# Two blocks' convolution moved from two to all four 64x64 tiles of TensorE

## The chip, the cores and the metric

The kernel runs on one core of one Trainium2 chip. The metric is the time of one execution in device microseconds (us).

## The reference, cut to what matters

A causal depthwise convolution with 7 taps per head (softmax over the taps), then a product, an exact GELU and a second product, for 8 x 4096 tokens of 192 channels.

```python
w = softmax(weight)                       # 8 heads x 7 taps, 24 channels a head
x_pad = concatenate([zeros(B, 6, D), x])  # per sequence
out[b, s, h] = sum_k w[h, k] * x_pad[b, s + k, h]
...
h = out.reshape(32768, 192) @ w_in        # 192 x 2048
g = 0.5 * h * (1 + erf(h / sqrt(2)))
return g @ w_out                          # 2048 x 192
```

## The kernel before

Tokens are halved over partitions: partitions 0 to 63 hold 64 channels of the first half of the tokens, partitions 64 to 127 the same channels of the second half. Three channel groups p = 0, 1, 2 lie along the free axis. Work goes in blocks n; the first six have 256 tokens a half. For all blocks but the two first, VectorE does the convolution. For blocks 0 and 1 TensorE does it, as 7 accumulating matmuls per group and half, each with the diagonal 64x64 matrix of one tap. I call the matmuls that stand together behind one product a bundle. `win` and `wout` are the two weight matrices in SBUF, `xc` holds the result of the convolution, and the halo is the 6 tokens before a block that its taps reach back to.

```python
def pconv(n, p, k):                      # TensorE: group p, tap k of block n
    ...                                  # waits for the cast, the diagonals, the halo
    for hf in range(2):                  # token half = row half = column half
        r = slice(64 * hf, 64 * hf + 64)
        ins = t.matmul(
            bank(CONVB[n][p], r, w), dg[r, d0 : d0 + 64], xTb[PC[n]][r, x0 : x0 + w],
            start=(k == KS - 1), stop=(k == 0),
            tile_position=(64 * hf, 64 * hf),
        )
    if k == 0:
        ins.then_inc(S_PC)

for p in range(NP):                      # block 1's groups go behind products 4, 5, 6 of block 0
    behind[0, 4 + p] = [(1, p, k) for k in range(KS - 1, -1, -1)]
```

Two of the four tiles work: (0, 0) and (64, 64). The results are copied from PSUM to `xc`, by ScalarE for block 0 and by VectorE for block 1. VectorE is one queue in order, and the place of block 1's copies in it matters below:

```python
diag(0); diag(1)                         # diagonals of groups 0 and 1
for p in range(NP): trans(0, p)
diag(2)                                  # diagonals of group 2
dup(0)                                   # two copies of win's first slice
dup(1); dup(2)
for p in range(NP): trans(1, p)
for p in range(NP): cast(1, p)

# copy p of block 1 stands before operation 0, 3 or 5 of block 2;
# operations 0 to 2 of block 2 are its transposes, which wait for its load
side = [((2, (0, 3, 5)[p]), conv_out, 1, p) for p in range(NP)]
```

The first product of block n (`mm1`, line 703) needs all of `xc`; it is followed by GELUs on ScalarE (line 631) and by the second product (line 734 or 767), which needs `wout`.

Of the kernel before, what the change touches and what calls it, by code (L numbers as in the profile page):

```python
# [6 lines left out]
AF = mybir.ActivationFunctionType  # L7
# [4 lines left out]
def bass_lightweight_conv__then__act_gelu_exact_kernel(  # L12
# [8 lines left out]
    H, KS = weight.shape  # L21
# [7 lines left out]
    TB = 512  # L29
# [4 lines left out]
    PC = {0: 0, 1: 1}  # L34
# [66 lines left out]
    def sem(name):  # L101
        return es.enter_context(nc.semaphore(name))
# [4 lines left out]
    with es:  # L107
# [37 lines left out]
        S_CAST = [sem("S_CAST%d" % i) for i in range(len(PC))]  # L145
        S_PC = sem("S_PC")
        S_PCE = sem("S_PCE")
        S_DUPE = sem("S_DUPE")
        S_HALO = sem("S_HALO")
        S_TR = sem("S_TR")  # L150
# [12 lines left out]
            return ob[r, 512 * (b % 4) : 512 * (b % 4) + w]  # L163


        CONVB = {0: [0, 1, 2], 1: [3, 0, 1]}

        NCV = NP * KS
        FQ = F // 8
# [3 lines left out]
        def cvd(n):  # L173

            return NCV * sum(m not in PC for m in range(n + 1))

        def pce(n, p):

            return NP * PC[n] + p + 1


        HC = [0]
# [156 lines left out]
        @block.gpsimd  # L339
        def _(g):  # L340
            def win_in(c0, c1, sm):
                for hf in range(2):
                    g.dma_start(  # L343
                        ap(win, 64 * hf * NP * F + c0, [[NP * F, 64], [F, NP], [1, c1 - c0]]),
                        ap(wint, hf * FH + c0, [[NP * F, 64], [F, NP], [1, c1 - c0]]),
                    ).then_inc(sm, 16)

            g.wait_ge(S_MSET, 1)
            for hf in range(2):
                m = idb[64 * hf : 64 * hf + 64, :]  # L350
                g.affine_select(
                    out=m,
                    in_=m,
                    compare_op=ALU.is_equal,
                    fill=0.0,
                    base=0,
                    pattern=[[-1, 64]],
                    channel_multiplier=1,
                ).then_inc(S_IDN)
            for i in range(3):  # L360
                win_in(FP[i], FP[i + 1], S_WIN[i])

            def halo(n):
                if n == 0:

                    t = xTb[0]
                    g.memset(
                        ap(t, 0, [[NP * XB, 128], [XB, NP], [32, HB]]), 0.0
                    ).then_inc(S_HALO)
                    for p in range(NP):  # L370
                        g.wait_ge(S_TR, p + 1)
                        g.tensor_copy(
                            ap(t, p * XB + 1, [[NP * XB, 128], [32, HB], [1, 31]]),
                            ap(
                                xT[0],
                                p * XW + HX + WS[0] - HL,
                                [[NP * XW, 128], [32, HB], [1, 31]],
                            ),
                        ).then_inc(S_HALO)
                    return  # L380

                t, tw = (xTb[1], XB) if n in PC else (xT[n % 2], XW)
                dst = ap(t, HF, [[NP * tw, 128], [tw, NP], [1, HB]])
                if n >= 2:
                    if n - 2 in PC:
                        g.wait_ge(S_PCE, pce(n - 2, NP - 1))
                    else:
                        g.wait_ge(S_CV, cvd(n - 2))
                if OFF[n] % SEQ == 0:
                    g.memset(dst, 0.0).then_inc(S_HALO)  # L390
                    return
                g.wait_ge(S_TR, NP * n)
                if n == 1:
                    src = ap(
                        xT[0],
                        HX + WS[0] - HL + 31,
                        [[NP * XW, 128], [XW, NP], [32, HB]],
                    )
                else:
                    src = ap(  # L400
                        xT[(n - 1) % 2],
                        HF + WS[n - 1],
                        [[NP * XW, 128], [XW, NP], [1, HB]],
                    )
                g.tensor_copy(dst, src).then_inc(S_HALO)  # L405

            g.wait_ge(S_IDN, 2)
            halo(0)
            g.dma_start(
                ap(wout, 0, [[NF * C, 128], [C, NF], [1, C]]),  # L410
                ap(woutt, 0, [[C, 128], [128 * C, NF], [1, C]]),
            ).then_inc(S_WOUT, 16)
            halo(1)
            for n in range(2, NB):
                halo(n)

        @block.vector
        def _(v):
# [62 lines left out]
                    ap(xT[n % 2], p * XW + HX, [[NP * XW, 128], [1, WS[n]]]),  # L481
                ).then_inc(S_CAST[PC[n]])

            def conv_out(n, p):
                v.wait_ge(S_PC, pce(n, p))
                v.tensor_copy(
                    xc[n % 2][:, p * TB : p * TB + WS[n]], bank(CONVB[n][p], w=WS[n])
                ).then_inc(S_PCE)

            def trans(n, p):  # L490
                w = WS[n]
                if p == 0:
                    if xin_at(n) > 0:
                        v.wait_ge(S_XIN[n % NX], xin_at(n))
                    if n >= 2 and n - 2 in PC:
                        v.wait_ge(S_PCE, pce(n - 2, NP - 1))
                    elif n >= 2:
                        v.wait_ge(S_CV, cvd(n - 2))
                    if n >= 1:
                        v.wait_ge(S_HALO, HC[n])  # L500
                v.transpose(  # L501
                    ap(xT[n % 2], p * XW + HX, [[NP * XW, 128], [1, w]]),
                    ap(
                        xin[n % NX],
                        p,
                        [[TB // 32 * DQ, 128], [D if n == 0 else DQ, w // 32], [NP, 32]],
                    ),
                ).then_inc(S_TR)
# [38 lines left out]
            diag(1)  # L547
            for p in range(NP):
                trans(0, p)
            diag(2)  # L550
            dup(0)
            dup(1)
            dup(2)
            for p in range(NP):
                trans(1, p)
            for p in range(NP):
                cast(1, p)

            side = [((2, (0, 3, 5)[p]), conv_out, 1, p) for p in range(NP)]
            for n in range(M0, M1):  # L560
                for j, at in enumerate([(n + 2, 18), (n + 3, 6), (n + 3, 9)]):
                    side.append((at, evac_t, v, n, j))
# [16 lines left out]
        def _(a):  # L579
# [10 lines left out]
                accum_out=wsm[:, 0:1],  # L590
            ).then_inc(S_ACTP)
            a.activation(out=hot[:, 1:2], in_=warm[0:1, 0:1], func=AF.Gelu).then_inc(S_HOT)
            for p in range(NP):
                a.wait_ge(S_TR, p + 1)
                a.activation(  # L595
                    out=ap(xTb[0], p * XB + HL, [[NP * XB, 128], [1, WS[0]]]),
                    in_=ap(xT[0], p * XW + HX, [[NP * XW, 128], [1, WS[0]]]),
                    func=AF.Copy,
                ).then_inc(S_CAST[0])
            for p in range(NP):  # L600
                a.wait_ge(S_PC, p + 1)
                a.activation(
                    out=xc[0][:, p * TB : p * TB + WS[0]],
                    in_=bank(CONVB[0][p], w=WS[0]),
                    func=AF.Copy,
                ).then_inc(S_PCE)

            due = {(1, 6): [(0, 0)]}
            for m in range(NA):
# [32 lines left out]
        def _(t):  # L642
# [1 line left out]
            for i in range(16):  # L644
                t.matmul(hp[1][:, 0:512], warm[:, 0:128], warm[:, :])  # L645

            def pconv(n, p, k):

                w = WS[n]
                if k == KS - 1:  # L650
                    t.wait_ge(S_CAST[PC[n]], p + 1)
                    if n == 0:
                        t.wait_ge(S_DG, p + 1)
                if k == KS - 2:
                    t.wait_ge(S_HALO, HC[n] + 2 + p if n == 0 else HC[n + 1])
                for hf in range(2):
                    r = slice(64 * hf, 64 * hf + 64)
                    d0 = (p * KS + k) * 64
                    x0 = p * XB + (32 * k if n == 0 else HF + k)
                    ins = t.matmul(  # L660
                        bank(CONVB[n][p], r, w),
                        dg[r, d0 : d0 + 64],
                        xTb[PC[n]][r, x0 : x0 + w],
                        start=(k == KS - 1),
                        stop=(k == 0),
                        tile_position=(64 * hf, 64 * hf),
                    )
                if k == 0:
                    ins.then_inc(S_PC)

            taps = [(p, k) for p in range(NP) for k in range(KS - 1, -1, -1)]
            for p, k in taps:
                pconv(0, p, k)

            behind = {}
            for p in range(NP):
                behind[0, 4 + p] = [(1, p, k) for k in range(KS - 1, -1, -1)]

            def mm1(n, i):
                w, c = WS[n], NCH[n]  # L680
# [2 lines left out]
                    t.wait_ge(S_GELU, u - 1)  # L683
                if i == 0:
                    if n in PC:
                        t.wait_ge(S_PCE, pce(n, NP - 2))
                    else:
                        t.wait_ge(S_CV, cvd(n))
                if n == 0 and i in (0, 2, 4):
# [2 lines left out]
                for cc in range(c):  # L692
                    f0 = 128 * CH[i * c + cc]
                    for p in range(NP):
                        if n in PC and i == 0 and cc == 0 and p == NP - 1:
                            t.wait_ge(S_PCE, pce(n, p))
                        for hf in range(2):
                            r = slice(64 * hf, 64 * hf + 64)
                            fw = 64 if M0 < n <= M1 else 128
# [158 lines left out]
```

## Time and profile before

| | before |
|---|---|
| median of the first 3 runs | 686.01 us (685.57 to 686.14) |
| profiled run | 684.97 us, span 683.2 us |
| TensorE busy | 676.7 us, 99% of the span |
| convolution matmuls | 84, 5.3 us busy |
| first GELU starts | 11.04 us |
| first use of `wout` | 20.32 us |

Times in the profile are counted from the start of the span. Those of the table are from the timeline; in a chain a piece counts only from the end of the piece before it, so its start can lie up to 0.2 us later (20.49 for the 20.32 here). A line of the timeline gives start, us, engine, line, operation, output and input, and in brackets the idle time before it and what ended it.

```profile
17.15 1.33 DVE L501 STREAM_TRANSPOSE xT<-xin 128x256 f32<-128x256 f32 x3 [0.90 <-DMA xin<-in_x_dram]
...
19.23 0.42 DVE L486 CAST xc<-ob 128x256 bf16<-128x256 f32 x1
```

The transposes of block 2 wait 0.90 us for a load, and the last copy of block 1 stands behind them. Here the copy ends at 19.65 and TensorE does not wait for it: the wait costs nothing in this run.

### The profile page before, as it was taken

How to read it: one execution, taken by the hardware profiler on the slowest of the kernel's cores; microseconds unless marked ns; L12 is line 12 of the kernel's file. 1: busy time of each engine (PE TensorE's matmuls, PEld its weight loads, DVE VectorE, ACT ScalarE, POOL GpSimd, SP SyncE). 2: the span in 40 equal slices, each digit the busy share in tenths (PEclk: the TensorE clock that was granted, in tenths of full speed). 3: DMA queues.
4: the chain of work that ended last, by engine and by line, in shares of the span. 5: the costliest groups of instructions: out<-in, count | busy, mean ns of one | idle time of the engine just before them, and what ended most of it. 6: DMA issues, size and time to landing. Idle time of an engine off the chain costs nothing.

```text
span 683.2 us, 27246 instructions
## 1 busy us (share of the span) xinstructions
PE 676.7 (99%) x12548; PEld 411.2 (60%) x12548; DVE 564.3 (83%) x914; ACT 534.0 (78%) x540; POOL 20.4 (3%) x51
## 2 busy tenths in 40 slices
PE   8999999999999999999999999999999999999998
PEld 4899655555555555555555555555555555555557
DVE  6999979888889888898888898888898888988611
ACT  6788987777787877777877878777778777778772
POOL 4000000000000000000000000000000000000000
PEclk9999999999999999999999999999999999999999
DMA  9345422244431244432334422344422444320123
GB/s 180 74 108 121 91 60 57 46 89 95 94 91 46 55 94 95 94 78 41 73 94 95 94 61 46 84 95 95 93 49 51 94 95 95 76 47 23 48 49 94
DMA packets 133970, 54.00 MB, mean 79 GB/s; under 512 B 128480, under 2 KB 133728, under 8 KB 133856
## 3 DMA queue, kind: packets, MB, share of 16 engines
q1 hardware_dynamic: 129872, 49.93, 32.1%
q0 software_dynamic: 3312, 1.57, 1.8%
q8 instruction: 98, 1.61, 1.0%
q10 hardware_dynamic: 672, 0.76, 0.4%
q14 instruction: 16, 0.13, 0.1%
HBM read 28.66 MB, written 25.17 MB: 79 GB/s over the span
## 4 chain that ended last, share of the span: by engine, by line
PE 96%; ACT 2%; DVE 1%; issue 0%; DMA 0%; ACTq 0%
PE hp L703 48%; PE ob L767 42%; PE ob L734 5%; ACT gT L631 2%; PE ob L660 1%; DMA wsb<-in_weight_dram 0%; DVE dg L453 0%; ACT osb L228 0%; DVE wcol L445 0%; DVE osb L270 0%; DVE xT L501 0%; ACT xTb L595 0%; ACT wex L585 0%; DVE osb L239 0%; DVE wch L439 0%
## 5 line engine op out<-in xcount | busy, mean ns | idle before, releaser
L631 ACT ACTIVATE gT<-hp 128x1024 bf16<-128x1024 f32 x512 | 523.4, 1024 | 132.7 <-PE hp L703 129.5
L703 PE MATMUL hp<-xc,win 64*64 64x512 bf16 (+2 forms) x6048 | 418.9, 366 | 1.0 <-ACT gT L631 0.7
L767 PE MATMUL ob<-gT,wout 64*64 64x512 bf16 x5376 | 366.7, 376 | 0.0
L531 DVE SCALAR_TENSOR_TENSOR acc<-xT,wcol,acc 128x512 f32<-128x512 f32 (+1 forms) x495 | 315.0, 710 | 0.0
L703 PEld LDWEIGHTS hp<-xc,win 64*64 64x64 bf16 (+1 forms) x6048 | 188.8, 106 | 134.7 <-ACT gT L631 2.3
L767 PEld LDWEIGHTS ob<-gT,wout 64*64 64x64 bf16 x5376 | 173.3, 118 | 121.7
L270 DVE STREAM_TRANSPOSE osb<-ob 128x512 f32<-128x512 f32 x84 | 74.4, 889 | 101.4 <-PE ob L767 101.4
L501 DVE STREAM_TRANSPOSE xT<-xin 128x512 f32<-128x512 f32 (+1 forms) x105 | 78.5, 807 | 0.9 <-DMA xin<-in_x_dram 0.9
L531 DVE SCALAR_TENSOR_TENSOR xc<-xT,wcol,acc 128x512 bf16<-128x512 f32 (+1 forms) x99 | 65.2, 716 | 0.0
L734 PE MATMUL ob<-wout,gT 64*128 64x192 bf16 x1024 | 52.2, 243 | 0.3
L734 PEld LDWEIGHTS ob<-wout,gT 64*128 64x128 bf16 x1024 | 43.6, 94 | 6.3 <-PE ob L734 0.6
L524 DVE TENSOR_SCALAR acc<-xT,wcol 128x512 f32<-128x512 f32 (+1 forms) x99 | 40.7, 467 | 1.1
L405 POOL COPY xT<-xT 128x18 f32<-128x18 f32 x30 | 12.7, 423 | 531.2 <-DVE xT L501 525.4
L241 ACT ACTIVATE osb<-ob 128x192 f32<-128x192 f32 x4 | 1.3, 331 | 9.5 <-PE ob L734 9.5
L239 DVE COPY osb<-ob 128x192 f32<-128x192 f32 x4 | 1.4, 358 | 8.4 <-PE ob L734 8.4
L660 PE MATMUL ob<-xTb,dg 64*64 64x256 bf16 x84 | 5.3, 272 | 1.1 <-ACT xTb L595 1.1
L645 PE MATMUL hp<-warm 128*128 128x512 bf16 x16 | 5.0, 482 | 1.3 <-DVE warm L419 1.3
L228 ACT ACTIVATE osb<-ob 128x384 f32<-128x384 f32 x12 | 5.8, 485 | 0.0
L660 PEld LDWEIGHTS ob<-xTb,dg 64*64 64x64 bf16 x84 | 4.3, 107 | 2.3 <-ACT xTb L595 1.6
L645 PEld LDWEIGHTS hp<-warm 128*128 128x128 bf16 x16 | 1.8, 118 | 4.0 <-issue 1.9
L464 DVE COPY win<-win 64x768 bf16<-64x768 bf16 (+1 forms) x6 | 3.7, 620 | 0.2
L343 POOL DMA_DIRECT2D win<-in_moe_w_in_dram x6 | 3.9, 652 | 0.0
(31 smaller groups left out, 16.4 us busy)
## 6 DMA issues: line engine op xcount, KB each, us to landing
out_dram<-osb SPq DMA_DIRECT2D x122, 192.0 KB, 3.1
xin<-in_x_dram SPq DMA_DIRECT2D x116, 192.0 KB, 4.0
xin<-in_x_dram SPq DMA_DIRECT2D x20, 96.0 KB, 3.3
wout<-in_moe_w_out_dram POOLq DMA_DIRECT2D x1, 768.0 KB, 10.3
win<-in_moe_w_in_dram POOLq DMA_DIRECT2D x4, 96.0 KB, 4.1
win<-in_moe_w_in_dram POOLq DMA_DIRECT2D x2, 192.0 KB, 4.7
out_dram<-osb SPq DMA_DIRECT2D x8, 48.0 KB, 1.7
out_dram<-osb ACTq DMA_DIRECT2D x4, 96.0 KB, 2.1
```

Of the source, the lines that this page charges most:

```text
L228: e.activation(out=dst, in_=src, func=AF.Copy).then_inc(S_EVA)
L270: v.transpose(ap(osb[m % 2], j, [[8 * C, 128], [C // 2, TB // 32], [NP, 32]]), bank(ring(m, j)),).then_inc(S_EV)
L405: g.tensor_copy(dst, src).then_inc(S_HALO)
L501: v.transpose(ap(xT[n % 2], p * XW + HX, [[NP * XW, 128], [1, w]]), ap(xin[n % NX], p, [[TB // 32 * DQ, 128], [D if n == 0 else DQ, w // 3 ...
L524: ins = v.tensor_scalar(a, src, wk, None, ALU.mult)
L531: ins = v.scalar_tensor_tensor(dst, src, wk, a, op0=ALU.mult, op1=ALU.add)
L631: a.activation(out=ap(gT[n % 2], i * c * 2 * w, dst), in_=ap(hp[u % 2], 0, src), func=AF.Gelu,).then_inc(S_GELU)
L645: t.matmul(hp[1][:, 0:512], warm[:, 0:128], warm[:, :])
L660: ins = t.matmul(bank(CONVB[n][p], r, w), dg[r, d0 : d0 + 64], xTb[PC[n]][r, x0 : x0 + w], start=(k == KS - 1), stop=(k == 0), tile_positi ...
L703: ins = t.matmul(hp[u % 2][fo : fo + fw, o : o + w], win[r, f1 : f1 + fw], xc[n % 2][r, p * TB : p * TB + w], start=(p == 0), stop=(p == N ...
L734: ins = t.matmul(bank(bb[sub], w=C), gT[m % 2][r, c0 : c0 + 128], wout[r, CH[i] * C : (CH[i] + 1) * C], start=(ph == 0 and i == 0), stop=( ...
L767: ins = t.matmul(bank(ring(m, j), slice(64 * h, 64 * h + 64), w), ap(wout, 64 * hf * NF * C + CH[i] * C + j, [[NF * C, 64], [NP, 64]],), g ...
```

## The change

The intent is to use the two idle tiles. Groups 0 and 1 run side by side: group 0 on the straight tiles, group 1 on the crossed ones, where the first token half's result lands in the second half's partitions and the other way round. The copies out of PSUM put the halves back. Group 2 is cut in two parts of 128 columns, one straight and one crossed. With six pieces to copy instead of three, the copies are shared anew: in block 0 ScalarE takes four and VectorE the two crossed ones of group 1. ScalarE also builds group 2's diagonals, which VectorE did before. In block 1 all six copies stay on VectorE, and they now stand ahead of block 2's transposes. The code is cut where `...` stands.

```diff
+        def kinds(n):
+            w = WS[n]
+            return [(0, 0, 0, w), (1, 1, 0, w), (2, 0, 0, w // 2), (2, 1, w // 2, w // 2)]
+        PIECES = [(0, None), (1, 0), (1, 1), (2, None), (3, 0), (3, 1)]
+        PA = (0, 3, 4, 5)
 ...
             for p in range(NP):
                 trans(0, p)
-            diag(2)
             dup(0)
+            conv_out(v, 0, 1)
+            conv_out(v, 0, 2)
             dup(1)
             dup(2)
 ...
             for p in range(NP):
                 cast(1, p)
-
-            side = [((2, (0, 3, 5)[p]), conv_out, 1, p) for p in range(NP)]
+            for j in range(len(PIECES)):
+                conv_out(v, 1, j)
+
+            side = []
 ...
+            for k in range(KS):          # ScalarE: diagonals of group 2
+                a.activation(out=dg[:, d0 : d0 + 64], in_=idb[:, :], func=AF.Copy,
+                             scale=wcol[:, c0 : c0 + 1]).then_inc(S_DGA)
 ...
                 for hf in range(2):
+                    ho = hf ^ ex
-                        bank(CONVB[n][p], r, w),
+                        bank(kd, slice(64 * ho, 64 * ho + 64), w),
-                        tile_position=(64 * hf, 64 * hf),
+                        tile_position=(64 * hf, 64 * ho),
 ...
+            order = [0] * 4 + [1, 0] * 3 + [1, 2] * 4 + [3, 2] * 3 + [3] * 4
 ...
+            behind = {
+                (0, 4): [(1, kd, k) for k in taps for kd in (0, 1)],
+                (0, 5): [(1, kd, k) for k in taps for kd in (2, 3)],
+            }
```

More of the change, by code (lines that the diff above doesn't have):

```diff
@@ L147, in bass_lightweight_conv__then__act_gelu_exact_kernel @@
         S_PCE = sem("S_PCE")
+        S_PCA = sem("S_PCA")
+        S_DGA = sem("S_DGA")
         S_DUPE = sem("S_DUPE")
@@ L163, in bank, with conv_out, wait_pc @@
             return ob[r, 512 * (b % 4) : 512 * (b % 4) + w]
-        CONVB = {0: [0, 1, 2], 1: [3, 0, 1]}
+        def kinds(n):
[3 more added lines that the diff above has]
+        PA = (0, 3, 4, 5)
+        def conv_out(e, n, j):
+            kd, h = PIECES[j]
+            p, ex, c0, w = kinds(n)[kd]
+            e.wait_ge(S_PC, 4 * PC[n] + kd + 1)
+            ro = slice(0, 128) if h is None else slice(64 * h, 64 * h + 64)
+            ri = ro if not ex else slice(64 - 64 * h, 128 - 64 * h)
+            dst = xc[n % 2][ro, p * TB + c0 : p * TB + c0 + w]
+            src = bank(kd, ri, w)
+            if n == 0 and j in PA:
+                e.activation(out=dst, in_=src, func=AF.Copy).then_inc(S_PCA)
+            else:
+                e.tensor_copy(dst, src).then_inc(S_PCE)
+        def wait_pc(e, n, p):
+            if n == 0:
+                e.wait_ge(S_PCA, (1, 1, len(PA))[p])
+                if p >= 1:
+                    e.wait_ge(S_PCE, 2)
+            else:
+                e.wait_ge(S_PCE, 2 + (1, 3, 6)[p])
         NCV = NP * KS
@@ L175, in cvd @@
             return NCV * sum(m not in PC for m in range(n + 1))
-        def pce(n, p):
-            return NP * PC[n] + p + 1
         HC = [0]
@@ L385, in halo @@
                     if n - 2 in PC:
-                        g.wait_ge(S_PCE, pce(n - 2, NP - 1))
+                        wait_pc(g, n - 2, NP - 1)
                     else:
@@ L482, in cast @@
                 ).then_inc(S_CAST[PC[n]])
-            def conv_out(n, p):
-                v.wait_ge(S_PC, pce(n, p))
-                v.tensor_copy(
-                    xc[n % 2][:, p * TB : p * TB + WS[n]], bank(CONVB[n][p], w=WS[n])
-                ).then_inc(S_PCE)
             def trans(n, p):
@@ L495, in trans @@
                     if n >= 2 and n - 2 in PC:
-                        v.wait_ge(S_PCE, pce(n - 2, NP - 1))
+                        wait_pc(v, n - 2, NP - 1)
                     elif n >= 2:
@@ L592, in _ @@
             a.activation(out=hot[:, 1:2], in_=warm[0:1, 0:1], func=AF.Gelu).then_inc(S_HOT)
+            a.wait_ge(S_PRO, 10)
+            a.wait_ge(S_IDN, 2)
+            for k in range(KS):
+                d0 = ((NP - 1) * KS + k) * 64
+                c0 = (NP - 1) * 32 + k
+                a.activation(
+                    out=dg[:, d0 : d0 + 64],
+                    in_=idb[:, :],
+                    func=AF.Copy,
+                    scale=wcol[:, c0 : c0 + 1],
+                ).then_inc(S_DGA)
             for p in range(NP):
@@ L599, in _ @@
                 ).then_inc(S_CAST[0])
-            for p in range(NP):
-                a.wait_ge(S_PC, p + 1)
-                a.activation(
-                    out=xc[0][:, p * TB : p * TB + WS[0]],
-                    in_=bank(CONVB[0][p], w=WS[0]),
-                    func=AF.Copy,
-                ).then_inc(S_PCE)
+            for j in PA:
+                conv_out(a, 0, j)
             due = {(1, 6): [(0, 0)]}
@@ L645, in _, with pconv @@
                 t.matmul(hp[1][:, 0:512], warm[:, 0:128], warm[:, :])
-            def pconv(n, p, k):
-                w = WS[n]
+            def pconv(n, kd, k):
+                p, ex, c0, w = kinds(n)[kd]
                 if k == KS - 1:
@@ L652, in pconv @@
                     if n == 0:
-                        t.wait_ge(S_DG, p + 1)
+                        if p < NP - 1:
+                            t.wait_ge(S_DG, p + 1)
+                        else:
+                            t.wait_ge(S_DGA, KS)
                 if k == KS - 2:
@@ L656, in pconv @@
                 for hf in range(2):
+                    ho = hf ^ ex
                     r = slice(64 * hf, 64 * hf + 64)
                     d0 = (p * KS + k) * 64
-                    x0 = p * XB + (32 * k if n == 0 else HF + k)
+                    x0 = p * XB + (32 * k if n == 0 else HF + k) + c0
                     ins = t.matmul(
-                        bank(CONVB[n][p], r, w),
+                        bank(kd, slice(64 * ho, 64 * ho + 64), w),
                         dg[r, d0 : d0 + 64],
@@ L669, in pconv @@
                     ins.then_inc(S_PC)
-            taps = [(p, k) for p in range(NP) for k in range(KS - 1, -1, -1)]
-            for p, k in taps:
-                pconv(0, p, k)
-            behind = {}
-            for p in range(NP):
-                behind[0, 4 + p] = [(1, p, k) for k in range(KS - 1, -1, -1)]
+            taps = range(KS - 1, -1, -1)
+            seq = {kd: [(0, kd, k) for k in taps] for kd in range(4)}
+            order = [0] * 4 + [1, 0] * 3 + [1, 2] * 4 + [3, 2] * 3 + [3] * 4
+            for kd in order:
+                pconv(*seq[kd].pop(0))
+            behind = {
+                (0, 4): [(1, kd, k) for k in taps for kd in (0, 1)],
+                (0, 5): [(1, kd, k) for k in taps for kd in (2, 3)],
+            }
             def mm1(n, i):
@@ L685, in mm1 @@
                     if n in PC:
-                        t.wait_ge(S_PCE, pce(n, NP - 2))
+                        wait_pc(t, n, NP - 2)
                     else:
@@ L695, in mm1 @@
                         if n in PC and i == 0 and cc == 0 and p == NP - 1:
-                            t.wait_ge(S_PCE, pce(n, p))
+                            wait_pc(t, n, p)
                         for hf in range(2):
```

## The prediction

> **What bounds the kernel now.** I read the page first (busy shares, chain, groups), then the chain in order of time over the first 21 us, then the same stretch engine by engine, because the change touches only the two first blocks of 256 tokens a half.
>
> ```profile
> PE 676.7 (99%) x12548; PEld 411.2 (60%) x12548; DVE 564.3 (83%) x914; ACT 534.0 (78%) x540; POOL 20.4 (3%) x51
> PE 96%; ACT 2%; DVE 1%; issue 0%; DMA 0%; ACTq 0%
> L660 PE MATMUL ob<-xTb,dg 64*64 64x256 bf16 x84 | 5.3, 272 | 1.1 <-ACT xTb L595 1.1
> ```
>
> TensorE sets the time: 99% busy, 96% of the chain, full clock. The matmuls that the change rewrites (L660, the convolution as diagonal matmuls) are 84 of 12548 and 5.3 us of 683.2. So 5.3 us, 0.8%, bounds what their work can give: a verdict past 2% is out of reach unless something stalls for over 13 us. What remains is the sign and size of a change of about 1 us. Every shift of TensorE early on reaches the end one for one, as the later chain is PE behind PE; the wait on GELUs near 73 to 82 us is relative to earlier work and moves along.
>
> The chain of the first 21 us (start, us, what):
>
> ```profile
> 5.33 1.16 DVE dg L453 x2
> 6.50 0.44 DVE xT L501
> 6.96 0.42 ACT xTb L595
> 7.42 2.48 PE ob L660 x42
> 9.96 0.40 PE hp L703 x4
> 10.38 0.63 PE hp L703 x8
> 11.04 1.94 ACT gT L631 x2
> 12.99 1.03 ACT gT L631
> 14.07 0.83 PE hp L703 x12
> 14.89 0.88 PE ob L660 x14
> 15.78 0.76 PE hp L703 x12
> 16.54 0.88 PE ob L660 x14
> 17.43 0.76 PE hp L703 x12
> 18.19 0.88 PE ob L660 x14
> 19.07 1.42 PE hp L703 x24
> 20.49 0.50 PE ob L734 x12
> ```
>
> The reader should see three stages. Block 0's convolution runs 7.42 to 9.90 and releases the first product (9.96; its last third waits for the last copy until 10.38). From 11.04 to 14.07 three GELUs of about 1.0 us each set the pace. From 14.07 to 20.49 it is TensorE again: product, convolution of block 1, product, and so on.
>
> The other engines meanwhile:
>
> ```profile
> 8.28 3.88 DVE L464 COPY win<-win 64x768 bf16<-64x768 bf16 x6
> 9.95 0.39 ACT L602 ACTIVATE xc<-ob 128x256 bf16<-128x256 f32 x1 [0.38 <-PE ob L660]
> 18.41 0.39 DVE L486 CAST xc<-ob 128x256 bf16<-128x256 f32 x1
> SPq L288 <- DMA wout<-in_moe_w_out_dram: 7.9, 1, 7.9
> ```
>
> VectorE duplicates win without a gap from 8.28 to 12.16. A copy out of PSUM takes 0.39 us for 256 columns. The sync queue's wait on wout ends when its next load is issued at 18.68, so wout has landed by then; the first second-product matmul (20.32) does not wait for it now.
>
> **What the Trainium skill says.** "TensorE: Matmul & The Clock Gate", Part 3 (The mechanism), says matmuls on different tiles run concurrently with starts about 4 ns apart. The trace agrees for two tiles: 42 matmuls of 256 columns in 2.48 us are 59 ns each, 118 ns a pair, against about 107 ns for one stream of 256 columns at 2.4 GHz. The same page, Part 1 (Wait — 56ns, not 53.3ns?), gives a floor of about 25 ns between matmul starts; nothing in the trace is dense enough to test it (the closest are the 64x192 matmuls, 41 ns apart in 12 per 0.50 us). "ScalarE: Activation LUTs", What ACT_TABLE_LOAD costs, says that a per-partition pointer operand adds about 93 ns to an activation and that activations back to back overlap by about 93 ns. The trace: 0.20 us for 1x1 without a pointer, 0.30 for 8x7 with one, and five GELUs of 1.02 in 4.92 us, an overlap nearer 50 ns. "SBUF — State Buffer", on the shared port pair, says VectorE in its two-port modes and GpSimd lock each other out. The trace fits: the second win copy takes 1.06 us while GpSimd generates wout's descriptors, its like 0.45.
>
> **The change, part by part.**
>
> (a) Work on TensorE. Two whole groups (kinds 0 and 1, 256 columns) now run on the straight and the crossed tiles, and the third group is cut into two of 128 columns. Per block 56 matmuls instead of 42. If a set of four takes what a pair takes now, that is 118/4 = 29.5 ns each. I use it for the 128-column ones too, as half of it would pass the 25 ns floor. So 28 matmuls cost 28 x 29.5 = 0.83 us, what 14 cost now (14 x 59 = 0.83), and a block costs two such bundles, not three.
>
> (b) Seven activations on ScalarE build the last diagonals. Each: 0.20 + 0.10 for the pointer + 64 columns x 0.85 ns (from (417 - 200)/256) = 0.355, less 50 to 93 ns of overlap, so 0.26 to 0.31 us; seven take 1.85 to 2.1 us from 5.35, when wcol is ready. They end at about 7.3, but the first cast could start at 6.96: 0.34 us late. The three casts, 0.37 apart, end near 8.4 instead of 8.2.
>
> (c) Block 0. TensorE starts at 7.76 instead of 7.42: 4 pairs alone 0.47, 3 sets of four 0.36 (8.59), 4 sets 0.48 (9.07, kind 1 done), 3 sets 0.36 (9.43, kind 2 done), 8 matmuls of kind 3 0.24, end 9.67. VectorE, without its third diagonal, starts win's first two copies at 7.7 instead of 8.28; at the 1.54 us they take now they end at 9.25. Then the two crossed copies, 0.42 each: 9.67 and 10.09. ScalarE's 128-column copies (0.20 + 128 x 0.85 ns = 0.31 with rounding and release) end near 10.3. So the first product starts near 10.1 instead of 9.96, its last third near 10.3 instead of 10.38, and the first GELU near 10.95 instead of 11.04. Gain here: about 0.1 us only. 0.8 us less on TensorE goes to the late start and to the copies.
>
> (d) The GELU-paced stretch is unchanged in length, so the fifth product starts at T = 13.97.
>
> (e) Block 1, from T, with the durations of the chain above: product 0.82, bundle 0.88, product 0.76, bundle 0.88, product 0.76 (T+4.10), product 0.66 (T+4.76). The product after that needs the GELU of the product that ended at T+4.10: 1.02 us from T+4.14, to T+5.16. So TensorE waits 0.4 us, then 0.7 for the product: T+5.9. Before, the same point was 20.49 - 14.07 = 6.42 after T. Gain 0.5 us; the 1.0 us of the removed bundle is half turned into a wait on ScalarE.
>
> (f) Off the path: VectorE's six copies of block 1 end near T+4.2 = 18.2, before their use at T+5.2. Block 2's transposes move from 17.15 to about 18.2, its convolution ends near 27, where TensorE needs it near 30. The first use of wout moves to about 19.9, over a microsecond after landing.
>
> Sum: 0.1 + 0.5 = 0.6 us, 686.0 to 685.4 us.
>
> **Rivals.** First, weight loads limit four tiles. A 64x64 load shows a median of 107 ns, as long as 256 columns stream, and the pairs already run 11 ns over the stream. If loads of the two tiles of one row half cannot overlap, a set of four takes two pairs' time: 56 matmuls at 59 ns are 3.3 us against 2.5 now, and the kernel becomes about 1 us slower (687). Against it: the later 64x64 products run on four tiles at 54 ns a matmul with the same loads, so loads come at least that often there; but that is at 512 columns and proves no more. Second, block 0's copies arrive later than I think: the last halo copy on GpSimd meets win's copies on VectorE and not the diagonal, so it may be locked out (it took 0.65 us already, its siblings 0.34), holding the third group and then everything by 0.3 to 0.5 us: 685.8. Third, the four tiles run at their ideal and block 0's chain profits (activations overlapping fully, kind 3 at 13 ns): 1.3 to 1.5 us faster, 684.6. Fourth, earlier TensorE runs into wout's landing at 18.68: this caps any gain near 1.6 us.
>
> **Range and chances.** The sum is a tenth of a per cent; the runs of before alone span 0.57 us. Rivals one and three lie about 1 to 1.5 us to either side, rival one the less likely. I take 684.5 to 686.4 as holding it 8 times in 10. A change past 2% needs 13.7 us and I see no mechanism of that size: 1% faster, 98% same, 1% slower.
>
> **What would show it.** The convolution group should show 112 matmuls, with block 1's in two bundles of near 0.9 us. 1.5 us or more a bundle means rival one. The first cast of block 0 should start near 7.3 with ScalarE busy before it, and the first GELU between 10.7 and 11.2. The chain near 19 us should show a GELU between the last product of block 0 and the first of block 1; if it shows PE only, step (e) is wrong. A TensorE wait on wout or on a halo copy would show rivals four and two. A difference after 30 us that is not this early shift would break the argument that the rest only moves along.

## More of the kernel before

The profiled run was faster than any of the timed ones.

## The result, and the profile after

The changed kernel took 683.94 us (median of 4, 683.70 to 684.11) against 685.79 (median of 4, 685.48 to 686.14) of the kernel before. The ratio is 0.9973, with a 95% interval of 0.9955 to 0.9990. Ratios here are not quite the ratio of the medians or means quoted. The gain of about 1.85 us is three times what I predicted, and the time lies below my range (684.5 to 686.4). Over all chips the kernel before has 45 runs with a mean of 685.70 us and the changed one 14 with 683.87: 1.83 us, with a standard error of 0.1.

The page of the changed kernel, the engines' busy time and the convolution's group:

```profile
PE 674.9 (99%) x12576; PEld 407.5 (60%) x12576; DVE 564.4 (83%) x918; ACT 535.7 (79%) x548; POOL 20.3 (3%) x51
...
L696 PE MATMUL ob<-xTb,dg 64*64 64x256 bf16 (+1 forms) x112 | 3.3, 246 | 0.7 <-ACT xTb L632 0.7
```

112 matmuls are busy for 3.3 us where 84 took 5.3. TensorE's busy time fell by 1.8 us. The chain of the first stretch (start, us, what):

```profile
5.27 1.78 ACT dg L624 x7
7.05 0.31 ACT xTb L632
...
7.41 1.52 PE ob L696 x40
...
8.95 0.28 ACT xc L188
...
9.75 0.84 PE hp L743 x12
...
10.62 1.94 ACT gT L663 x2
...
13.64 0.83 PE hp L743 x12
14.47 0.89 PE ob L696 x28
15.36 0.76 PE hp L743 x12
16.12 0.52 PE ob L696 x28
16.64 0.78 PE hp L743 x12
...
17.45 1.03 ACT gT L663
...
18.52 0.83 PE hp L743 x12
19.35 0.50 PE ob L774 x12
```

The first GELU starts at 10.62 instead of 11.04 (0.42 us). From the fifth product to the first use of `wout` it is 19.35 - 13.64 = 5.71 us instead of 6.42 (0.71 us). A GELU stands between the last product of block 0 and the first of block 1, as predicted. After that the two chains run in step but for 0.15 us gained at the next product, which before still waited for a GELU. A second product that began at 83.78 us begins at 82.50, and the last of all at 669.67 instead of 670.96: 1.28 and 1.29 us. What is gained early moves along unchanged.

So the two traces differ by 1.3 us and the timed medians by 1.85. VectorE's timeline of the changed kernel:

```profile
7.71 0.87 DVE L493 COPY win<-win 64x768 bf16<-64x768 bf16 x2
8.77 0.88 DVE L190 CAST xc<-ob 64x256 bf16<-64x256 f32 x2 [0.19 <-PE ob L696]
...
15.40 2.30 DVE L190 CAST xc<-ob 128x256 bf16<-128x256 f32 x6 [1.47 <-PE ob L696]
17.73 1.33 DVE L524 STREAM_TRANSPOSE xT<-xin 128x256 f32<-128x256 f32 x3
```

The two win copies take 0.87 us where they took 1.54, and block 1's six copies are done at 17.70, ahead of the transposes.

### The profile page after: what moved, and what is told of

Its sections match the earlier page's. It is cut to its first block, busy times and chain, and to the rows that moved or that the text cites. A ratio compares the mean times of both kernels' runs of the same rounds, so it can differ in the third digit from the quotient of the medians. Undisturbed runs are those within 1.5% of the kernel's fastest.

```text
span 681.9 us, 27319 instructions
## 1 busy us (share of the span) xinstructions
PE 674.9 (99%) x12576; PEld 407.5 (60%) x12576; DVE 564.4 (83%) x918; ACT 535.7 (79%) x548; POOL 20.3 (3%) x51
## 4 chain that ended last, share of the span: by engine, by line
PE 96%; ACT 3%; issue 0%; DVE 0%; ACTq 0%
PE hp L743 47%; PE ob L807 43%; PE ob L774 6%; ACT gT L663 2%; PE ob L696 0%; ACT dg L624 0%; ACT osb L257 0%; DVE wcol L474 0%; DVE osb L299 0%; ACT L607 0%; ACT xc L188 0%; ACTq L317 0%; DVE osb L268 0%; ACT wex L611 0%; ACT xTb L632 0%
## 5 line engine op out<-in xcount | busy, mean ns | idle before, releaser
L190 DVE CAST xc<-ob 64x256 bf16<-64x256 f32 (+3 forms) x8 | 3.0, 373 | 1.8 <-PE ob L696 1.7
L696 PE MATMUL ob<-xTb,dg 64*64 64x256 bf16 (+1 forms) x112 | 3.3, 246 | 0.7 <-ACT xTb L632 0.7
L696 PEld LDWEIGHTS ob<-xTb,dg 64*64 64x64 bf16 x112 | 2.6, 106 | 1.7 <-ACT xTb L632 1.2
```

Of the source, the lines that this page charges most:

```text
L696: ins = t.matmul(bank(kd, slice(64 * ho, 64 * ho + 64), w), dg[r, d0 : d0 + 64], xTb[PC[n]][r, x0 : x0 + w], start=(k == KS - 1), stop=(k ...
```

## The experiments

All outputs are right. Experiments of one group ran on one chip, with nine runs of the kernel before beside them. Several kernels were made from a copy of the changed one with switches; the diffs are cut, and show in the code or in words what the switch does.

### The kernel before and the changed kernel again

No edit. First group, five rounds each.

> The kernel before, unchanged, against itself: it shows what differences of a few tenths of a us mean. Theory A (the gain is what the two traces show, about 1.3 us; the rest of the 1.85 us between the timed medians is from run to run) expects single runs to spread by 0.5 us or more and the ratio to be 1.000 within 0.0007. Theory B (the gain is 1.85 us, a part of it where the traces do not show it) expects runs that agree within 0.3 us.

> The changed kernel, unchanged, five rounds. Theory A expects 1.2 to 1.5 us less than the kernel before (ratio 0.9978 to 0.9983); theory B 1.7 to 2.0 us (ratio 0.9971 to 0.9975).

The kernel before against itself came out at a ratio of 1.0004 (0.9992 to 1.0017), but its 14 runs spread from 684.92 to 686.68 us. The five runs of the changed kernel lie between 683.72 and 684.10; median 683.88, ratio 0.9974 (0.9960 to 0.9987). So the kernel before varies by 1.8 us and the changed one by 0.4 us. Theory A was right that the kernel before spreads; theory B was right in the number and wrong about the spread. The interval of this one ratio holds both theories' numbers; what decides is that the first result and the last group agree with it (0.9973 both; 1.83 us over all runs). Neither theory had said that only one of the two kernels spreads. The profiled run here took 686.12 us, and its VectorE timeline shows why:

```profile
18.64 1.33 DVE L501 STREAM_TRANSPOSE xT<-xin 128x256 f32<-128x256 f32 x3 [2.43 <-DMA xin<-in_x_dram]
...
20.71 0.42 DVE L486 CAST xc<-ob 128x256 bf16<-128x256 f32 x1
```

Block 2's load came 1.5 us later than in the first trace, and block 1's last copy with it: 20.71 instead of 19.23. The first use of `wout` moved from 20.32 to 21.63 us, and the span from 683.2 to 684.4. The trace on which I had built the prediction was one of the lucky runs.

The second trace of the changed kernel is the counterpart. There block 2's load was even later, and VectorE waited for it:

```profile
19.00 1.34 DVE L524 STREAM_TRANSPOSE xT<-xin 128x256 f32<-128x256 f32 x3 [1.06 <-DMA xin<-in_x_dram]
```

But the six copies had ended at 17.94, and TensorE did not wait: the first use of `wout` came at 19.52 us (19.19 in the first trace), and the run took 684.08 us.

### Block 0 alone, block 1 alone

First group. Block 0 alone keeps block 1's two tiles, its three bundles and its copies behind block 2's transposes. Block 1 alone keeps block 0 as before.

```diff
 # block 0 alone, against the changed kernel; block 1 alone is the mirror of it
-  kinds(1): (0,0,0,w) (1,1,0,w) (2,0,0,w/2) (2,1,w/2,w/2)
+  kinds(1): (0,0,0,w) (1,0,0,w) (2,0,0,w)
-  six copies of block 1 before block 2's transposes
+  three copies of block 1 at operations 0, 3 and 5 of block 2
```

> Block 0 on four tiles with its copies and the diagonals on ScalarE, block 1 as before. From the traces: the first GELU at 10.6 us instead of 11.0, a gain of 0.4 us that lasts to the end (theory A). My prediction's step (c) said 0.1 us. If the two parts do not add, block 0 alone gives less than 0.2 us because the vector queue reaches block 1 no earlier.

> Block 1 on four tiles, block 0 as before. From the traces: 6.42 us between the fifth product and the first second-product become 5.7, and 0.15 us more just after, so 0.85 us of gain (theory A); my prediction's step (e) said 0.5 us. Rival: the wait on the GELU takes more of it when block 0 is late, and less than 0.5 us is left.

Block 0 alone: 685.63 us (685.08 to 686.64), ratio 1.0000 (0.9987 to 1.0012): no gain that the runs can show, and the spread of the kernel before is still there. Its first GELU does start at 10.63 us; theory A was wrong that this lasts. Its chain, near the product that follows:

```profile
10.18 7.32 DMA xin<-in_x_dram
...
20.08 0.61 PE hp L777 x8
```

The chain runs through block 2's load, the transposes and the copies to the first product of block 1. The 0.4 us won earlier are lost waiting there.

Block 1 alone (with its copies ahead of the transposes): 684.40 us (684.34 to 684.55), ratio 0.9981 (0.9969 to 0.9994), mean 1.2 us below the kernel before, and the spread is gone. It gave more than the 0.85 us expected, although its trace's first GELU was 0.3 us late (11.34; the 16 warm-up matmuls ended at 7.80 there).

### The copies' place alone

Third group. The kernel before with its three copies ahead of the transposes; and the changed kernel with its six copies put where the kernel before has its three.

```diff
 # the first: kernel before
-            side = [((2, (0, 3, 5)[p]), conv_out, 1, p) for p in range(NP)]
+            for p in range(NP):
+                conv_out(1, p)
+            side = []
 # the second: changed kernel
-            for j in range(len(PIECES)):
-                conv_out(v, 1, j)
-            side = []
+            side = [((2, (0, 3, 3, 5, 5, 5)[j]), conv_out, v, 1, j) for j in range(len(PIECES))]
```

> The kernel before with one edit: VectorE's three copies of block 1 come before block 2's transposes, not between them and block 2's convolution; the convolution stays on two tiles. Theory Q (in the kernel before, two of these copies queue behind transposes that wait for block 2's load, and that load lands anywhere from 17.1 to 18.6 us; this order is a part of the change's gain that my prediction left out) expects every run near the fastest of the kernel before, 684.9 to 685.3 us, with a spread below 0.5 us, where the kernel before runs from 684.9 to 686.7. Theory R (the spread comes from the start-up or from later) expects the same spread as the kernel before, 1 us or more.

> The changed kernel with one edit: block 1's six copies at the places that the kernel before gives its three (one before block 2's transposes, two behind them, three behind two more instructions). Theory Q expects the first product of block 1 to wait for these copies in every run: copies done at 20.7 us if the load lands at 17.1, at 22 if at 18.6, against 18.2 in the change, so 685.2 to 687 us, spread 1 us or more: the four tiles' whole gain gone. Theory R expects 683.9 us as the change.

The first ran at 685.11 us (684.91 to 685.21), ratio 0.9988 (0.9975 to 1.0000). The kernel before beside it ran from 685.01 to 686.92, mean 685.84. With a spread of 0.3 us and a mean of 685.06 this is theory Q: the order of the copies alone, on two tiles, removes the slow runs. Only 16 of the 45 runs of the kernel before lie at 685.3 us or below; all five of these do. On the mean it is worth 0.8 us beside the runs of its own chip (the interval of that ratio ends at 1.0000), and 0.6 us against all 45. Its profile shows the last copy waiting for TensorE's matmuls and no longer behind a load:

```profile
19.10 0.42 DVE L486 CAST xc<-ob 128x256 bf16<-128x256 f32 x1 [1.22 <-PE ob L663]
```

In this run `wout` landed only at 20.59 us, and TensorE waited 0.16 us for it; the first use was at 20.64.

The second ran at 688.62 us (688.19 to 689.25), ratio 1.0041 (1.0028 to 1.0053): 2.8 us slower than the kernel before, and some 4.7 us slower than the change. The direction is theory Q's, the size is above its range. The chain shows copies that end at 22.76 us, and the stretches of 4 us (busy us of each engine, then clock, DMA share, GB/s) show what the estimate lacked:

```profile
18.00:22.00 4.00, 1.31 (x22) 0.65 (x16) 2.87 (x8) 1.97 (x3) 0.00 (x0) 1.00 0.23 44
22.00:26.00 4.00, 3.19 (x38) 2.54 (x40) 3.91 (x12) 1.05 (x2) 0.20 (x1) 0.57 0.72 171
```

TensorE worked 1.31 of the 4 us while it waited, and in the next 4 us its granted clock was 0.57 on average. So the wait is paid once as a wait and again as slow matmuls (the 8 of the product behind it took 1.03 us, 0.61 in the chain of block 0 alone). The load also landed later here, at 19.0 us, than in either trace of the kernel before. The run shows what the place costs in sum; it does not part these three.

### The diagonals back on VectorE

Second group. The changed kernel, but `diag(2)` is on VectorE again, before win's first copies.

```diff
             for p in range(NP):
                 trans(0, p)
+            diag(2)
             dup(0)
 ...
-            for k in range(KS):          # ScalarE: diagonals of group 2
-                a.activation(... scale=wcol[:, c0 : c0 + 1]).then_inc(S_DGA)
```

> The change with the third group of diagonals back on VectorE, behind the transposes. Theory M (moving the diagonals is a main part of block 0's gain: it lets win's first two copies run before GpSimd generates wout's descriptors and lets the crossed copies start at 8.8 us) expects the two win copies to take about 1.5 us again instead of 0.87, the crossed copies to start after 9.8 us and the first GELU at 11.1 us or later, so most or all of the 0.4 us is lost. Theory N (the shorter convolution is the gain, the diagonals only make room) expects a first GELU within 0.2 us of 10.6.

It ran at 684.87 us (684.82 to 684.94), some 0.9 to 1.1 us slower than the changed kernel's medians on other chips; the first GELU started at 11.64 us. That is theory M, and by more than the 0.4 us that it had at stake: block 0 on four tiles without the moved diagonals is later than the kernel before. Its chain:

```profile
8.71 1.06 DVE win L514
...
9.80 0.42 DVE xc L206
```

The second win copy takes 1.06 us again. It starts at 8.71 us, 0.36 us into GpSimd's generation of descriptors (the orders for a transfer) for `wout`, which runs for 1.20 us from 8.35, and the crossed copies come after it. In the changed kernel the two win copies start at 7.71, are through at 8.58, and take 0.87 us together. But the second of them does not run before the descriptors there, as theory M had it: these are generated from 8.15, and the copy starts at 8.16 and takes 0.42 us. So the traces show that this copy is quick when it starts with the descriptors and slow when it starts 0.36 us into them. Of the crossed copies' delay (8.77 to 9.80), 0.52 us is VectorE's later start on win, for the diagonals, and 0.67 the slower win copies; 0.19 comes off, for which the change waits for TensorE there.

### Block 1's second bundle later

Second group, and again in the last one.

```diff
-                (0, 5): [(1, kd, k) for k in taps for kd in (2, 3)],
+                (0, 6): [(1, kd, k) for k in taps for kd in (2, 3)],
```

> The change, with block 1's second bundle one product later (behind the seventh product, not the sixth). If the wait on a GELU before the first product of block 1 is real and costs 0.45 us, then moving the bundle lets that GELU start about 0.5 us earlier and fills the wait with the bundle: 0.3 to 0.5 us faster than the change. Rival: VectorE's copies then come too late (three copies of about 0.28 us behind the bundle) and the wait only changes its name: within 0.1 us of the change.

It ran at 683.48 us (683.42 to 684.34): three runs near 683.4 and two near 684.3. The chain of the profiled run, one of the fast ones, shows the wait on a GELU turned into two GELUs back to back that start earlier:

```profile
16.19 1.95 ACT gT L689 x2
```

The first use of `wout` is at 18.95 us instead of 19.19. The three quick runs are some 0.45 us below the changed kernel's medians on other chips, the size expected; the trace's first use of `wout` is only 0.24 us earlier, and on one chip with the changed kernel, in the last group, the mean was no better (683.86 against 683.76). What the slower runs waited for is taken up below.

### The rate of a bundle by itself

Second group, one round. One of block 1's bundles is done five times over, each time from a fresh start of the accumulation, so the result is the same.

```diff
-                (0, 4): [(1, kd, k) for k in taps for kd in (0, 1)],
+                (0, 4): 5 * [(1, kd, k) for k in taps for kd in (0, 1)],   # semaphore in the last only
 # the other kernel: the same with (2, 3), the matmuls of 128 columns
```

> The change with block 1's first bundle (28 matmuls of 256 columns on four tiles) done five times over; the result is the same. Measures the rate without the switch of tile shape: at 107 ns a set of four each more bundle takes 0.75 us (26.7 ns a matmul), by my prediction's 29.5 ns 0.83 us, under serial weight loads 1.5 us.

> The change with block 1's second bundle (28 matmuls of 128 columns on four tiles) done five times over; the result is the same. At the streaming rate each more bundle takes 0.37 us (13.3 ns a matmul); with the floor of 25 ns per matmul that my prediction used, 0.70 us; with 29.5 ns 0.83 us.

The chain shows the bundles of 256 columns, then, in the other kernel, those of 128:

```profile
14.47 4.14 PE ob L722 x140
```
```profile
16.24 2.09 PE ob L722 x140
```

One bundle of 256 columns took 0.89 us, five took 4.14: (4.14 - 0.89) / 4 = 0.81 us a bundle, 29.0 ns a matmul, where the prediction used 29.5. Of 128 columns: (2.09 - 0.52) / 4 = 0.39 us, 14.0 ns a matmul, where the prediction used 29.5 as well. The whole runs took 686.86 and 685.73 us. Rival one of the prediction, weight loads that hold four tiles to the time of two pairs (59 ns a matmul), is out at both widths.

### Group 2 in one piece

Third group. Groups 0 and 1 as in the change; group 2 stays 256 columns wide on the straight tiles.

```diff
-            return [(0, 0, 0, w), (1, 1, 0, w), (2, 0, 0, w // 2), (2, 1, w // 2, w // 2)]
+            return [(0, 0, 0, w), (1, 1, 0, w), (2, 0, 0, w)]
```

> The change without the split of the third group: it stays one group of 256 columns on the two straight tiles (42 matmuls a block), groups 0 and 1 exchange halves as in the change. If 128-column sets really pass the 25 ns floor (14.0 ns a matmul in the run with the bundle repeated), the split is worth 0.88 - 0.52 = 0.36 us in block 1, less what it costs in two more copies; 683.9 + 0.3 = 684.2 us. With the floor that my prediction assumed, the split would be worth nothing: 683.9 or less, as there are fewer copies.

It ran at 684.46 us (684.21 to 684.80), about 0.5 us slower than the change on other chips. In its chain the second bundle takes 0.88 us and the stretch from the fifth product to the first use of `wout` 19.79 - 13.71 = 6.08 us, 0.37 more than in the change. So the cut of group 2 pays 0.37 us in block 1; in block 0 the first GELU (10.69) is not later than in the traces of the change (10.62 to 10.75).

### Where wout's landing caps the gain

The prediction's fourth rival. A first attempt, in the third group, took the kernel with the later bundle and issued block 2's load only when `wout` had landed.

```diff
-            load(sp, 2)
             sp.wait_ge(S_WOUT, 16)
+            load(sp, 2)
             load(sp, 3)
```

> The version with the later bundle, with block 2's load issued only when wout has landed. The version with the later bundle ran at 683.4 us in three runs and 684.3 in two; its first use of wout (18.95 us) is where wout lands (18.4 to 19.4 us over the traces). If wout's landing makes the slow runs, sharing the queues with one load less brings wout in near 17 us and all runs to 683.4 or less, spread below 0.3. Rival: block 2's load then lands so late (20 us or more) that VectorE's convolution of block 2 is late for its product at 29 us, and the time is 684 or more.

It ran at 687.67 us (687.27 to 688.28). The rival won: block 2's transposes started at 22.89 us, and TensorE waited for VectorE's convolution of block 2:

```profile
32.41 0.94 PE hp L777 x12
```

Its matmuls behind that wait took nearly twice their time (1.28 us for 12 where 0.65 is usual), with a mean granted clock of 0.70 from 34 to 38 us. About `wout` this run says little: with less to share it landed at 18.02 us, not near 17.

The last group put it another way: the kernel with the later bundle again, and a version in which `wout` is first used one product later, with the changed kernel as a yardstick on the same chip. `share` holds the weights by which block 0's second product is spread over the first products of block 1.

```diff
-            share = {1: [3, 4, 4, 4, 4, 4, 4, 4]}
+            share = {1: [0, 4, 5, 5, 5, 5, 4, 4]}
```

> The changed kernel again, as the yardstick on the same chip for the next two: 683.7 to 684.1 us, as in its other nine runs.

> The version with the later bundle again. Theory W (the first use of wout, now near 18.95 us, waits for wout in those runs where it lands late) expects runs of 683.4 and some up to 684.4; the other theory (chance in two runs) expects 683.4 throughout.

> The version with the later bundle, where the second product of block 0 starts one product later (after the second first-product of block 1, not the first), so wout is first used near 19.8 us instead of 18.95. Theory W expects the slow runs to be gone or fewer: spread below 0.4 us, 683.4 to 683.8 us (a tenth or two may go to a wait for a GELU). Otherwise the spread stays near 0.9 us.

The changed kernel: 683.73 us (683.72 to 683.83). The later bundle: 683.77 (683.55 to 684.34). The later bundle with the later use: 683.52 (683.47 to 683.66), ratio to the kernel before 0.9970 (0.9957 to 0.9982) where the change has 0.9973. The profiled run of the second was its slowest, 684.34 us, and TensorE's timeline names a wait:

```profile
19.78 0.67 PE L808 MATMUL ob<-wout,gT 64*128 64x192 bf16 x12 [0.27 <-DMA wout<-in_moe_w_out_dram]
```

With the later use the spread falls from 0.8 to 0.2 us. The direction is theory W's: the landing of `wout` caps what an earlier TensorE can win. But the wait is 0.27 of the 0.83 us by which this first use is later than in the quick trace (18.95). The rest was lost before: VectorE waited 0.96 us for a late part of `win`, and block 1's first bundle began 0.30 us later for that (14.73 against 14.43) and took 0.20 us longer. The cap begins right where the change stands: over the traces of the change `wout` had landed by 18.75, 18.84 and 19.21 us, the last of these 0.03 us before its first use. The last version ran below both kernels, the changed one by 0.2 us on the mean (683.54 against 683.76 on the same chip; none of its five runs is as slow as the changed kernel's quickest there).

## Why the prediction was right or wrong

The prediction was wrong in size: a gain of 0.6 us, with a range down to 684.5, where 683.94 came. Its frame held: the early shift that moves along to the end, the chain through the steps named. Of the 1.25 us that it missed, the two traces put 0.32 on step (c) and 0.36 on step (e); the rest, some 0.57, is in no step of it.

**The step that failed most: (f), and the base it rests on.** It put VectorE's six copies "off the path" and looked only at whether they come in time in the changed kernel. It did not see that the kernel before has its copies behind transposes that wait for a load, so the change takes a wait away. In the profiled run that wait happened to cost nothing; in the other trace of that kernel it moved the first use of `wout` by 1.3 us. The order alone is worth 0.8 us on the mean of one chip (685.06 against 685.84), and without it the four tiles make the kernel 2.8 us slower. The prediction's own "686.0" was a median with this wait in it, while its steps were worked out from a trace of 684.97 us without it. That the profiled run lay 1 us below the median of the timed ones, and 0.6 us below the fastest of them, was in front of me.

**Step (c), block 0: 0.1 us predicted, 0.42 in the trace.** Two terms were mis-sized. From step (b): seven activations took 1.78 us instead of 1.95 and the first cast did not wait for the last to end, so TensorE started at 7.41, not 7.76. And win's first two copies took 0.87 us, not the 1.54 carried over from a place in time 0.57 us later; so the crossed copies ended at 9.65 instead of 10.09. The run with the diagonals back on VectorE shows both the 1.06 us copy and the late first GELU come back. What makes the copy slow is not shown: in both kernels it runs while GpSimd generates descriptors, and only its start within them differs (0.01 and 0.36 us in). That the two engines lock each other out is argued, not tested alone. Rival two (the halo copy locked out) did not come: GpSimd's three casts took 1.1 us, less than the 1.3 before.

**Step (e), block 1: 0.5 us predicted, 0.71 in the trace and 0.15 just behind it.** The first bundle took 0.89 us (0.88 predicted). The second took 0.52 instead of 0.88, because I held 128-column matmuls to 29.5 ns and they take 14.0. The wait on a GELU came where it was said to.

**Rival three was the better prediction.** It said that activations overlap fully, that kind 3 takes 13 ns a matmul, and that block 0's chain profits, for 1.3 to 1.5 us. The traces show 93 ns of overlap, 14.0 ns and 0.42 us, and 1.28 us in sum. I had taken the sum of my more cautious terms as the centre.

**Do the parts add?** Order 0.8 us, block 1's tiles 684.42 against 685.06 (0.6 us), block 0 683.93 against 684.42 (0.5 us): 1.9 us, from groups on different chips. Measured directly, on the means of one group: 685.65 - 683.93 = 1.7. This is a split and no test: each part begins where the one before ends, so the sum must come out but for the 0.2 us between the kernel before on the two chips. Block 0's part counts only on top of the new order; alone it gave nothing. The traces, which leave out the lucky run's wait, put 0.86 us on block 1 and 0.42 on block 0.

**What stays open:** why block 2's load and `wout` land up to 2 us apart from one run to the next; and what makes the second win copy slow.

## What to carry to other kernels

Look for what stands behind a wait on a transfer in an in-order queue: a copy that others need belongs ahead of it, and moving it can be worth more than the arithmetic beside it. Before building on one trace, compare its time with the timed runs; if it lies at the edge of them, ask which wait in it was lucky. Do not carry a duration that is longer than its like (1.06 against 0.45 us here) to another place in time before you know what made it long.

## What the Trainium skill lacked or had wrong

- "TensorE: Matmul & The Clock Gate", Part 1 (Wait — 56ns, not 53.3ns?): the floor of about 25 ns between matmul starts does not hold across tiles. 128-column matmuls on four 64x64 tiles ran at 14.0 ns each, steadily, over 140 of them. Part 3's 4 ns between tiles is not at odds with that; the floor should say that it is for one tile.
- The same page, Part 2 (LDWEIGHTS) gives columns / 1.2 ns for a load, an estimate of 53 ns for 64 columns, and Part 3's list of what overlaps lets loads overlap running matmuls only in another row group (the same part also names a background weight buffer). Four loads went with every set of four matmuls, in 56 ns a set, two of them in each row half, where two such loads one after the other would take 107 ns: loads of one row half must overlap each other and running matmuls, or be shorter than that. The trace can't tell which; it records 107 ns for each.
- "TensorEngine Tiling (Array Packing)", Key Properties, says that a change of tiling mode drains the engine, and gives no cost. Here a bundle in another mode cost 0.08 us at its start with 256 columns (0.89 against 0.81 for the next) and 0.13 with 128 (0.52 against 0.39), and the product behind the first 0.11 us (0.76 against 0.65): about 0.2 us for there and back. That the change of mode is the cause was not tested apart.
- "ScalarE: Activation LUTs", What ACT_TABLE_LOAD costs, gives one figure, about 93 ns, for the overlap of activations back to back. It was right where my step (b) allowed as little as 50: seven activations of 334 ns mean in 1.78 us overlap by (7 x 334 - 1780) / 6 = 93 ns. But five GELUs of 1021 ns mean in 4.92 us, in the same trace, overlap by (5 x 1021 - 4920) / 4 = 46 ns. The first read SBUF and the second PSUM.
- No page that I read says how far the landing of the same transfer varies between executions. Over the traces here block 2's load let the transposes start at 17.15 us in one run of the kernel before and at 18.64 in another.
